# A first unit of two first blocks in place of three, a further unit for the other two, and three edits beside it

## The chip, the cores and the metric

The kernel runs on one core of one Trainium2 chip, in one launch. The metric is device time in microseconds (us); the median of three runs before the change is 285.51 us (285.26 to 285.83).

A core has a matmul engine (PE, with its weight loads as PEld), a vector engine (DVE), an engine for activations (ACT), a general one (POOL) and SP, which issues transfers. Each runs its own instructions strictly in the order in which they were written, and waits on the others through semaphores. Transfers run on 16 DMA engines; here SP's queue carries the inputs and outputs, POOL's queue the weights of the FFN, which are turned from 32-bit into 16-bit floats on the way.

## What is computed

For four batches of eight heads with 768 positions and a head width of 64: block-sparse causal attention, and a gated FFN on the result.

```python
k_chunks = k.reshape(B, H, nc, chunk, D)            # chunks of 32 keys, nc = 24
k_min, k_max = np.min(k_chunks, axis=3), np.max(k_chunks, axis=3)
ub = np.sum(np.maximum(q * k_min, q * k_max), axis=-1)   # a bound for each query and chunk
ub = np.where(causal, ub, -1e9)
top_chunks = np.argsort(ub, axis=-1)[..., -6:]      # six chunks a query
scores = scale * q @ k.T
scores = np.where(sel & (pos[:, None] >= pos[None, :]), scores, -1e9)
attn = softmax(scores) @ v
x = attn.transpose(0, 2, 1, 3).reshape(3072, 512)
out = (sigmoid(x @ w_gate) * (x @ w_val)) @ w_out   # 512 -> 1536 -> 512
```

## The kernel before

**Tiles and units.** The 768 positions of a batch are six blocks of 128. A query of a batch's first block sees at most four chunks, so all that it sees is chosen, and such a *first block* needs only causal attention within 128 keys (`first`). All other blocks need the bounds, the choice of six chunks (`choose`), and attention over all earlier blocks with a mask (`attend`). Work goes by *units* of three blocks, 384 tokens. Unit 0 (`u0`) is the first blocks of batches 0, 1 and 2; `u1` is blocks 1 to 3 of batch 0; `u2` is blocks 4 and 5 of batch 0 and the first block of batch 3; `u3` to `u7` go on through batches 1 to 3. Every unit gets its FFN: `ffn` for `u0` to `u3`, and `ffn_pair` for the pairs `u4`/`u5` and `u6`/`u7`, which uses seven half products in place of eight.

**Names.** A first block's loads are `kf0`, `kf1`, `qf0`, `qf1` (half the heads each) and `vf`; PE turns them (`kfT`, `qfT`), ACT or DVE casts them (`kf16`, `qf16`), PE writes a causal triangle into the score bank (`scm`) and adds the scores (`scf`), ACT takes the exponential (`expf`), PE multiplies by the values (`pvf`), DVE normalizes (`rzf`, `xf`), and PE turns the result (`xpsf`) into `xT`, the FFN's input. For blocks of batch 0 beyond the first, `k0_u1` and the like are loads, `kn`/`qn` a copy into another order, `kT`/`qT` the turns, `kx0`/`kx1` the chunk minima and maxima, `ub_u1` the bounds, `mx`, `ap`, `apt`, `hqm` the choice; `sc`, `exp`, `cm`, `pv`, `x` and `xps` are the attention; `v_0_1` is a load of values and `v16_0_1` its cast on POOL. In the FFN, `g` and `v` are the two products of one of twelve column groups, `tanh` and `hg` their gating, `o0`, `o1`, `o2` thirds of the output projection of one token block, `osb` its copy out of PSUM, `out` the store. `wm` are 24 filler matmuls that keep PE busy early on. `wg`, `wv` and `wo` are the weight transfers, three each.

**The mask.** The extra 64 rows of the score product carry the choice: `hk` holds on these rows a fixed pattern that says which chunk a key belongs to. `pat` makes the pattern, `epat0` and `epat1` spread it to 768 columns, and four `hkp` copies put it into `hk`; every score product reads it.

**Order.** Nothing is scheduled on the chip. The program lists operations with their reads, writes and priorities, and a word list, `ORDER`, made beforehand by a planner, gives the order in which they are written, with the engine of an operation where there is a choice (`@ACT`) and the buffer slots (`:0`). The engines' own orders are the parts of this list. A load into a buffer waits for the last reader of that slot; `o0` of a token block waits for the transfer of the rows of `w_out` that it uses.

```python
def after(i, key, prio):      # a small POOL copy: what follows waits for a landed load
def weights(i, prio, after):  # wg{i}, wv{i}: 512 of 1536 columns each
def weights_out(i, prio, after):  # wo{i}: 4 of 12 row groups
```

`after0` waits for a load of the first block of batch 1, and `after1` for one of batch 2; `wg0` and `wv0` follow the first, the others the second.

Of the kernel before, what the change touches and what calls it, by code (L numbers as in the profile page):

```python
# [94 lines left out]
v10 q3_u1:0 pat0 kcr0 pat kf0_0:0 kf1_0 kf0_1:1 q0_u1 k3_u1 qn_u1_3@DVE:0 k1_u1 tri0 tri qf0_0:2 ident qf1_0 epat0:0  # L95
kfT_0:0 q2_u2:1 k0_u2 kf16_0:1 kxf1:0 qf1_1:3 qn_u1_0:2 kf1_1 ident16 kn_u1_3@DVE:3 wm_0:1 vf_0:4 kn_u1_1@DVE:4 wm_1
hkf1@DVE q2_u1 wm_2 kxf0 qf0_1 kT_u1_1:2 k0_u1 scm_0:3,4 qn_u2_2@POOL:5 kt_u1_1:0 k1_u2 qf0_2:5 hk0_u1_1@ACT qfT_0:5
q1_u2 hkp010@ACT kT_u1_3:6 qf1_2 qf16_0@DVE:6 kt_u1_3@DVE:1 q1_u1 v16_0_0 scf_0:0 kx1_u1_1:1 wm_3 hkf0 kf1_2:0
expf_0_1:1 hk0_u1_3 qT_u1_3:7 expf_0_0 kf0_2 kx0_u1_1 qfT_1:0 qn_u1_2:4 q0_u2 kx0_u1_3 wm_4 kn_u2_0:3 qf_u1_3:0
qT_u1_0:5 k2_u1 pvf_0_0:4 wm_5 hk1_u1_1@ACT qf_u1_0@DVE vf_1:2 pvf_0_1:3 wm_6 kn_u1_0:6 kn_u2_1@DVE:1 vf_2:4  # L100
qm_u1_0@POOL:0 hq1 qf16_1@DVE:0 kT_u1_0:2 k2_u2 kfT_1:7 kcr_f@POOL ap1 qm_u1_3@POOL qn_u1_1:2 scm_1:5,0 kx1_u1_3
kf16_1@DVE:6 after0 qT_u1_2:6 q3_u2 hk1_u1_3 qf_u1_2 scf_1:2 vf1_1:4 rzf_0_1:0 k3_u2 epat1@DVE:1 qT_u1_1:7 wg0
expf_1_0 wm_7 v_0_1:1 wm_8 expf_1_1:3 kn_u1_2@POOL:0 wm_9 v_0_3:3 qm_u1_2 kfT_2:6 kt_u1_0:0 wv0 kx1_u1_0 qf_u1_1
qfT_2:5 v_0_2:0 hq0_u1_0 rzf_0_0:1 kx0_u1_0 kT_u1_2:0 wm_10 after1 qm_u1_1@POOL kf16_2:6 kx0_u1_2 vc_1@ACT xf_0_0:0
wg1 kx1_u1_2 hq0_u1_1 xpsf_0_0:7,0 pvf_1_0:2 scm_2:6,4 wv1 rzf_1_0:1 qf16_2:2 kt_u1_2@DVE:1 xf_1_0:1 scf_2:1 vf1_2:0
hq0 pvf_1_1:5 kcr_u1 wm_11 expf_2_0 xTf_0_0 qn_u2_1@POOL:2 ub_u1:0,2 qn_u2_0@DVE:6 wg2 vc_2@ACT k01_1:0 ap0 expf_2_1:0
rzf_1_1:1 xf_1_1:2 wv2 hkp001@ACT xf_0_1:0 pvf_2_0:7 pvf_2_1:6 qT_u2_0:5 rzf_2_0:0 ubn1_u1:0 wm_12 hkp000@POOL wm_13
ubm1_u1 xpsf_0_1:4 qf_u2_0@DVE:1 wm_14 wm_15 xTf_0_1 hkp011@ACT wm_16 rzf_2_1:1 xpsf_1_1:3 xf_2_1:0 wm_17 wm_18
kn_u2_2@DVE:4 hq1_u1_2@POOL wm_19 xf_2_0:2 xpsf_1_0:2 xpsf_2_1:5 ubn0_u1 wm_20 hq1_u2_0@POOL hk0_u1_2@ACT
hk0_u1_0@POOL ubm0_u1 mx0_u1:0 kn_u2_3:0 wo1 qn_u2_3:6 xTf_1_1@ACT xpsf_2_0:4 xTf_2_0 qT_u2_2:6 xTf_1_0 kT_u2_0:7  # L110
xTf_2_1@ACT qT_u2_1:0 wm_21 ap0_u1 apt0_u1:0 mx1_u1 hqm0_u1_2 k00_1 qf_u2_1@DVE kT_u2_3:4 kt_u2_3:2 qf_u2_2 qT_u2_3:3
qf_u2_3 kT_u2_2:2 g_u0_0:5,0,0 wm_22 tanh_u0_0 v_u0_0:6 hqm0_u1_0 kx0_u2_3 hk1_u1_2@ACT hk1_u2_3 g_u0_1:3,1,1
hq1_u1_1@POOL kx1_u2_3:1 ap1_u1 sc_u1_1_0:0,2 qm_u2_0@POOL:0 tanh_u0_1 v_u0_1:5 hg_u0_0 qm_u2_2@ACT kx1_u2_2
g_u0_2:4,2,2 hq1_u1_0@POOL kt_u2_2@DVE:1 hq0_u1_2@POOL kx1_u2_0 v_u0_2:3 tanh_u0_2 apt1_u1 hq0_u1_3@POOL exp_u1_1_0
g_u0_3:6,3,3 kx0_u2_2 v16_0_1 hg_u0_1 sc_u1_0_1:4,3 wo0 v_u0_3:2 hg_u0_2 tanh_u0_3 hk0_u2_3@ACT hkp110 sc_u1_0_0:0
hk1_u1_0@POOL exp_u1_0_1 g_u0_4:5,0,4 exp_u1_0_0 kx0_u2_0 sc_u1_3_2:6,1 kt_u2_0@DVE:2 sc_u1_2_2:3,0 sc_u1_3_1:4
exp_u1_3_2 sc_u1_2_0:0 qm_u2_1 exp_u1_3_1 kT_u2_1:7 qm_u2_3 v_u0_4:6 exp_u1_2_0 kx1_u2_1 kx0_u2_1 sc_u1_3_0:4 cm_u1_2
g_u0_5:0,1,5 hg_u0_3 exp_u1_3_0 hkp100@POOL v_u0_5:2 kt_u2_1:0 hq1_u2_3 tanh_u0_5 g_u0_6:4,2,6 tanh_u0_4 hq0_u2_1@POOL
hg_u0_5 sc_u1_0_2:7 v_u0_6:0 kcr_u2@POOL exp_u1_0_2 hg_u0_4 cm_u1_3 hqm1_u1_2@ACT sc_u1_1_2:5 cm_u1_0 g_u0_7:2,3,7
v16_0_3 v_u0_7:7 tanh_u0_7 wo2 tanh_u0_6 g_u0_8:6,1,8 hg_u0_7 hq0_u2_3 cm_u1_1 ub_u2:2,4 hq1_u1_3@DVE tanh_u0_8  # L120
hq0_u2_0@POOL exp_u1_2_2 hk1_u2_0@POOL sc_u1_2_1:7 v_u0_8:6 hqm1_u1_0 exp_u1_2_1 k11_1 exp_u1_1_2 g_u0_9:3,0,9
hq1_u2_1@POOL hg_u0_8 v_u0_9:7 tanh_u0_9 sc_u1_1_1:5 g_u0_10:6,3,10 hg_u0_9 ubn1_u2:0 v_u0_10:3 v16_0_2 tanh_u0_10
exp_u1_1_1 g_u0_11:7,1,11 v11 hg_u0_10 pv_u1_3:4 ubn0_u2 tanh_u0_11 pv_u1_2 mx1_u2:0 pv_u1_0:6 hk0_u2_1@ACT
sc_u1_5_2:5,1 v_u0_11:3 hk0_u2_2 exp_u1_5_2 hg_u0_6 hk1_u2_2@ACT wm_23 hg_u0_11 pv_u1_1 sc_u1_6_1:1,3 sc_u1_5_0:2
hq0_u2_2@DVE exp_u1_6_1 sc_u1_7_1:7,0 rz_u1_1:0 sc_u1_5_1:5 x_u1_1:1 exp_u1_7_1 sc_u1_6_0:0 rz_u1_0:0 exp_u1_6_0
sc_u1_4_1:3,2 hkp101 exp_u1_5_0 sc_u1_4_0:1 o0_u0_0:4,0 kcr1 mx0_u2 k10_1 exp_u1_5_1 xps_u1_1:7,1 cm_u1_5 o1_u0_0
hq1_u2_2 ap1_u2 exp_u1_4_1 ap0_u2 sc_u1_7_0:0 x_u1_0:0 sc_u1_6_2:2 o2_u0_0 exp_u1_7_0 apt1_u2:0 exp_u1_6_2
hqm1_u2_0@DVE exp_u1_4_0 xps_u1_0:5 o0_u0_1:3,1 osb_u0_0@DVE cm_u1_4 apt0_u2 out_u0_0 o1_u0_1 cm_u1_6 hqm0_u2_2@ACT
cm_u1_7 sc_u1_4_2:6 pv_u1_5:0 hqm0_u2_0 q01_1:1 exp_u1_4_2 pv_u1_6:2 sc_u1_7_2:1 hqm1_u2_2 kf0_3:5 pv_u1_4 exp_u1_7_2
sc_u2_1_0:4,1 rz_u1_2:0 sc_u2_3_2:6,3 xT_u1_0 sc_u2_3_0:1 exp_u2_1_0 x_u1_2:2 pv_u1_7 o2_u0_1 exp_u2_3_0 cm_u2_1  # L130
rz_u1_3:0 x_u1_3:1 exp_u2_3_2 xT_u1_1 sc_u2_1_1:5 k16_1_2:5 sc_u2_2_0:4,2 kx1_1_3:0 exp_u2_1_1 sc_u2_7_1:0,0
xps_u1_3:1 q10_1 xps_u1_2:2 k16_1_3:3 exp_u2_2_0 sc_u2_3_1:6 k16_1_0@DVE:2 q00_1 o0_u0_2:7,0 osb_u0_1 cm_u2_3 kt_1_3:0
hk0_u2_0@ACT cm_u2_2 o1_u0_2 exp_u2_7_1 xT_u1_3 xT_u1_2@ACT kx0_1_0 o2_u0_2 v_0_4:2 kx1_1_0 g_u1_0:5,0,12 v_u1_0:4
kt_1_0:6 tanh_u1_0 g_u1_1:3,3,13 kx0_1_1 sc_u2_2_1:0 v_0_5:4 v_u1_1:1 exp_u2_2_1 hg_u1_0 q11_1 g_u1_2:2,2,14 tanh_u1_1
# [10 lines left out]
hg_u1_10 hk0_1_1@ACT sc_u2_6_1:3 mx1_u3 o0_u1_0:7,0 hqm0_u3_0@ACT hg_u1_11 o1_u1_0 rz_u2_1:0 ap1_u3 exp_u2_6_0
qf0_u4_1 x_u2_1:0 qfT_3:4 exp_u2_6_1 q00_2:1 cm_u2_6 apt1_u3 sc_u2_6_2:5 hq1_u3_2@ACT hqm0_u3_2 sc_u2_4_2:0 pv_u2_0
hk1_1_0 rz_u2_0:0 exp_u2_6_2 sc_u3_1_1:6,3 qf16_3@DVE:1 exp_u2_4_2 sc_u3_1_0:3 o2_u1_0 x_u2_0:1 cm_u2_4 exp_u2_4_1
kx0_2_2 o0_u1_1:5,1 hk1_1_2 osb_u1_0 exp_u3_1_0 hqm1_u3_0@DVE hk0_1_2 out_u1_0 pv_u2_7:4 kx1_2_3:0 pv_u2_4:0 v_1_3:4
xps_u2_1:2,0 sc_u2_5_1:1,0 v_1_2:1 xT_u2_1@ACT hkp111@POOL hqm1_u3_2@DVE exp_u3_1_1 scf_3:7,3,2 o1_u1_1 q10_2
# [1104 lines left out]
```

## Time and profile before

| | |
|---|---|
| median of three runs | 285.51 us |
| the profiled execution | 285.57 us |
| its span, first to last instruction | 283.7 us |
| PE, DVE, ACT, POOL busy | 95%, 83%, 73%, 41% of the span |
| read from and written to memory | 30.67 and 6.29 MB |

Times in the profile are microseconds from the span's start. A row of a timeline names the start, the duration, the engine, the line of the kernel, the operation, the tile written and the tiles read, and how many instructions are merged (x4). Matmuls are pipelined, so the duration of one (379 ns for 512 columns) is longer than the distance between two starts; distances say what PE can do. A row of a chain of waits gives the start, the length and the work that the end of the kernel hung on. "DMA to landing" is the time from issue until the data is there. The DMA share is a sum over packets in flight, divided by 16 engines, and can pass 1.

### The profile page before, as it was taken

The page shows a single profiled execution, that of the slowest core. Times are in us where ns is not written, and L with a number is a line of the kernel's source. Part 1 is how long each engine was busy: PE and PEld are TensorE (multiplying, and loading weights), DVE is VectorE, ACT ScalarE, POOL GpSimd, SP SyncE. Part 2 cuts the span into 40 slices and gives each one's busy share as a digit, 9 for nine tenths or more (in the row PEclk, how much of TensorE's full clock was granted, in tenths as well). Part 3 has the DMA queues.
Part 4 walks back from the last instruction along what each step waited for, and adds up shares of the span by engine and source line. Part 5 has one row for each costly group of instructions (what it writes and reads, how often), then busy time and mean ns, then how long its engine had stood idle before and what let it go on. Part 6 is the DMA issues. An engine that isn't in the chain of part 4 may idle for free.

```text
span 283.7 us, 7050 instructions
## 1 busy us (share of the span) xinstructions
...
## 2 busy tenths in 40 slices
...
DMA  6999999999999979999720143200001320200014
GB/s 173 254 252 201 196 200 216 167 206 178 229 171 183 199 154 159 217 168 227 166 54 2 31 116 94 64 14 2 0 0 31 104 91 12 76 0 0 2 73 149
DMA packets 130033, 34.26 MB, mean 121 GB/s; under 512 B 118096, under 2 KB 127056, under 8 KB 130000
## 3 DMA queue, kind: packets, MB, share of 16 engines
...
q8 instruction: 20, 0.33, 0.5%
q14 instruction: 13, 0.11, 0.1%
HBM read 30.67 MB, written 6.29 MB: 130 GB/s over the span
## 4 chain that ended last, share of the span: by engine, by line
PE 85%; DVE 4%; ACT 4%; issue 3%; POOL 2%; DMA 1%; DVEq 0%; POOLq 0%
PE o_u L981 22%; PE sc_u L862 11%; PE v_u L950 11%; PE g_u L950 11%; PE pv_u L895 6%; PE suv_u6u L1059 3%; PE sug_u6u L1059 3%; PE ube_u L801 3%; PE suv_u4u L1059 2%; PE sug_u4u L1059 2%; PE srg_u6u L1059 1%; PE srv_u6u L1059 1%; PE srv_u4u L1059 1%; PE srg_u4u L1059 1%; DMA kq_u<-in_q_dram 1%
## 5 line engine op out<-in xcount | busy, mean ns | idle before, releaser
L873 ACT ACTIVATE att_u<-sc_u 128x512 f16<-128x512 f32 (+3 forms) x184 | 90.4, 550 | 17.9 <-PE sc_u L862 17.0
L879 POOL TENSOR_SCALAR_AFFINE_SELECT att_u<-att_u 128x384 f16<-128x384 f16 (+1 forms) x56 | 28.5, 519 | 73.7 <-ACT att_u L873 52.4
L981 PE MATMUL o_u<-wo,hg_u 128*128 128x512 f16 x216 | 52.8, 379 | 0.0
L950 PE MATMUL v_u<-xT_u,wv 128*128 128x384 f16 x192 | 39.1, 326 | 0.1
L950 PE MATMUL g_u<-xT_u,wg 128*128 128x384 f16 x192 | 39.0, 326 | 0.0
L981 PEld LDWEIGHTS <-hg_u 128*128 128x128 f16 x216 | 20.0, 98 | 18.8 <-issue 0.6
L958 ACT ACTIVATE gate_u<-g_u 128x384 f16<-128x384 f32 x48 | 22.9, 494 | 11.0 <-PE g_u L950 9.3
L962 DVE SCALAR_TENSOR_TENSOR hg_u<-gate_u,v_u 128x384 f16<-128x384 f16 x48 | 25.1, 537 | 6.9 <-PE v_u L950 3.9
L862 PE MATMUL sc_u<-hqe,hke 128*128 128x128 f16 (+2 forms) x220 | 29.0, 243 | 0.0
L895 PEld LDWEIGHTS <-att_u 128*128 128x128 f16 x640 | 25.0, 98 | 4.9 <-issue 0.5
L862 PE MATMUL sc_u<-hqo,hko 128*128 128x128 f16 (+2 forms) x220 | 27.4, 243 | 0.0
L895 PE MATMUL pv_u<-v,att_u 128*128 128x65 f16 x640 | 27.2, 193 | 0.1
L950 PEld LDWEIGHTS <-wv 128*128 128x128 f16 x192 | 18.3, 98 | 10.9 <-issue 0.6
L950 PEld LDWEIGHTS <-wg 128*128 128x128 f16 x192 | 18.2, 98 | 10.6 <-issue 0.2
L862 PEld LDWEIGHTS <-hke 128*128 128x128 f16 x220 | 17.2, 98 | 7.3 <-issue 0.4
L862 PEld LDWEIGHTS <-hko 128*128 128x128 f16 x220 | 16.6, 98 | 6.5 <-issue 0.8
L567 POOL CAST v<-v 128x512 f16<-128x512 f32 x23 | 14.9, 662 | 12.4 <-DMA v<-in_v_dram 8.1
L990 ACT ACTIVATE osb_u<-o_u 128x512 f32<-128x512 f32 (+1 forms) x13 | 7.8, 597 | 13.9 <-PE o_u L981 13.9
L981 PE MATMUL o_u<-wo,hgp_u 128*128 128x512 f16 (+1 forms) x72 | 16.2, 370 | 0.0
L914 DVE TENSOR_TENSOR x_u<-pv_u,rz_u 128x384 f16<-128x384 f32 (+1 forms) x28 | 14.8, 531 | 0.4
L1059 PEld LDWEIGHTS <-Sv 128*128 128x128 f16 x96 | 9.0, 98 | 6.2 <-issue 0.3
L824 DVE MAX8 mx_u<-ubn_u 128x8 f32<-128x8 f32 (+16 forms) x152 | 12.6, 158 | 0.1
...
## 6 DMA issues: line engine op xcount, KB each, us to landing
v<-in_v_dram SPq DMA_DIRECT2D x23, 256.0 KB, 4.9
out_dram<-osb_u SPq DMA_DIRECT2D x23, 256.0 KB, 2.3
k<-in_k_dram SPq DMA_DIRECT2D x12, 384.0 KB, 5.8
q<-in_q_dram SPq DMA_DIRECT2D x12, 384.0 KB, 5.5
wg<-in_moe_w_gate_dram POOLq DMA_DIRECT2D x3, 512.0 KB, 10.8
wv<-in_moe_w_val_dram POOLq DMA_DIRECT2D x3, 512.0 KB, 13.4
wo<-in_moe_w_out_dram POOLq DMA_DIRECT2D x3, 512.0 KB, 12.8
kf<-in_k_dram SPq DMA_DIRECT2D x8, 128.0 KB, 3.9
```

Of the source, the lines that this page charges most:

```text
L567: plan.add(f"v16_{b}_{ib}", {POOL: pool(H * D)}, lambda e: nc.gpsimd.tensor_copy(v16[b % 2][:, ib, :, 0:D], at(t)), reads=[t], writes=[("v ...
L824: nc.vector.max(at(mx)[:, e_, j, :], at(ubn)[:, e_, j, 0:max(8, u.seen[j])])
L862: nc.tensor.matmul(at(t)[:, o:o + 128 * m], hk[b % 2][e_][:, p, 128 * jb:128 * jb + 128], hq[u.side][e_][:, p, 128 * x:128 * (x + m)], sta ...
L873: plan.add(f"exp_{u.name}_{h}_{y}", {ACT: act(n)}, lambda e, t=t, att=att, b0=b0, n=n: nc.scalar.activation(at(att)[:, b0:b0 + n], at(t), ...
L879: nc.gpsimd.affine_select(out=dv, in_=dv, compare_op=ALU.is_ge, fill=0.0, base=0, pattern=[[0, u.m], [1, 128]], channel_multiplier=-1)
L895: nc.tensor.matmul(at(pv)[:, last, x, :], at(att)[:, c:c + 128], v16[b % 2][:, jb, h, :], start=(jb == 0), stop=(jb == ib))
L914: plan.add(f"x_{u.name}_{p}", {DVE: dve(u.t)}, lambda e: nc.vector.tensor_tensor(at(x_).rearrange("p a (e d) -> p e a d", e=2), at(pv)[:, ...
L950: nc.tensor.matmul(at(t), w16[:, c, 128 * fb:128 * fb + 128], at(u.xt)[:, c, :], start=(c == 0), stop=(c == 3))
L958: plan.add(f"tanh_{u.name}_{fb}", {ACT: act(T)}, lambda e, g=g, gate=gate: nc.scalar.activation(at(gate), at(g), AF.Tanh, scale=0.5), read ...
L962: plan.add(f"hg_{u.name}_{fb}", {DVE: dve(T)}, lambda e, w_=w_, gate=gate, hg=hg: nc.vector.scalar_tensor_tensor(at(hg), at(gate), 1.0, at ...
L981: nc.tensor.matmul(at(o), hgs[c][1][1]()[:, 128 * tb:128 * tb + 128], wo16[:, fc, lo:hi], start=(c == 0), stop=(c == NFB - 1))
L1059: nc.tensor.matmul(at(t), left[i](c), right[i](c), start=first and c == 0, stop=c == 1, skip_group_check=not first)
```

## The change

Five things change at once, and the order list with them.

1. `u0` is the first blocks of batches 0 and 1 alone (256 tokens); a new unit `u8` holds the first blocks of batches 2 and 3; `u2` loses its third block. Their FFN products have 256 columns in place of 384, and there are three such units in place of two (with `u2`).
2. For the first blocks of batches 2 and 3 the triangle is put on after the exponential, by POOL (`cmf`), where before it was so for batch 3 alone.
3. The pattern for the mask is spread and copied in two column parts, chunks 0 to 7 and 8 to 23, so that `epat0` becomes `epat0a` and `epat0b`, and each `hkp0` an `a` and a `b`; a score product over the first four key blocks reads part `a`, and part `b` only where a key block beyond the fourth is used.
4. `w_out` comes in one transfer (`wo0`) in place of three, and every weight transfer follows `after0`.
5. The order list is a new one throughout, with new engines and slots.

```diff
     units = [
-        Unit(0, [], [(0, 0), (1, 1), (2, 2)]),
+        Unit(0, [], [(0, 0), (1, 1)]),
         Unit(1, [(0, 1), (0, 2), (0, 3)]),
-        Unit(2, [(0, 4), (0, 5)], [(3, 2)]),
+        Unit(2, [(0, 4), (0, 5)]),
...
+        Unit(8, [], [(2, 0), (3, 1)]),
     ]
...
+    PARTS = slice(0, 8), slice(8, NC)
...
+        for y, cut in enumerate(PARTS):
+            n = CH * (cut.stop - cut.start)
+            const(f"epat{o}{'ab'[y]}", {POOL: pool(n), DVE: dve(n, 1, 64), ACT: act(n, False, 64)}, lambda e, o=o, cut=cut: copy(
+                e, at(epat[o])[:, cut], pat[:, o, cut].unsqueeze(2).to_broadcast([64, cut.stop - cut.start, CH])),
+                reads=["pat"], writes=[(epat[o], y)], prio=-2.3)
...
-    def weights_out(i, prio, after):
-        return plan.add(f"wo{i}", {POOL: (760, 760)},
-                 lambda e: nc.gpsimd.dma_start(wo16[:, 4 * i:4 * i + 4, :], wos[:, 4 * i:4 * i + 4, :]),
-                 reads=after, writes=[("wo", i)], prio=prio, dma=(3000, 2048))
+    def weights_out(prio, after):
+        return plan.add("wo0", {POOL: (760, 760)}, lambda e: nc.gpsimd.dma_start(wo16, wos),
+                 reads=after, writes=[("wo", i) for i in range(3)], prio=prio, dma=(9000, 2048))
...
-        masked = b < 3
+        masked = b < 2
...
-                reads += [("hkp", b % 2, e_, p) for b, _, _, _ in u.banks[y]] + [("hq", u.side, e_, p), ("hqm", u.side, e_, p)]
+                reads += [("hkp", b % 2, e_, p, z) for b, jb, _, _ in u.banks[y] for z in range(1 + (jb > 3))] + [("hq", u.side, e_, p), ("hqm", u.side, e_, p)]
...
-            g = ps(f"g_{u.name}_{fb}", "ff", [128, T])
-            w_ = ps(f"v_{u.name}_{fb}", "ff", [128, T])
+            g = ps(f"g_{u.name}_{fb}", "ff", [128, u.w])
+            w_ = ps(f"v_{u.name}_{fb}", "ff", [128, u.w])
...
-    raw_f = {b: load_first(b, -10.0 + b) for b in range(3)}
+    raw_f = {b: load_first(b, -10.0 + b) for b in range(2)}
...
-    after(1, (raw_f[2]["q"], 1), -0.6)
     for i in range(1, 3):
-        weights(i, -0.5 + 0.2 * i, ["after1"])
-    for i in range(3):
-        weights_out(i, 0.3, ["after1"])
+        weights(i, -0.5 + 0.2 * i, ["after0"])
+    weights_out(0.3, ["after0"])
...
     ffn(units[0], 1.0, 0.95)
+    for b, x in units[8].first:
+        raw_f[b] = load_first(b, 0.05)
+        first(units[8], b, x, raw_f[b], 0.5)
+    ffn(units[8], 1.5, 0.5)
...
-    first(units[2], 3, 2, raw_f[3], 2.0)
```

The engines' orders at the start, read out of the two lists up to the first FFN product and a little beyond:

| | before | after |
|---|---|---|
| SP issues ahead of `g_u0_0` | 36 | 28 |
| SP from its 24th issue on, after | | `vf_0 vf_1 q3_u2 k00_1 v_0_3 v_0_2 qf0_2 kf0_2 vf_2 kf1_2 qf1_3 qf1_2 kf0_3 kf1_3 qf0_3 v_0_1 k01_1` |
| POOL around the weights, before | `qm_u1_3 after0 vf1_1 wg0 kn_u1_2 wv0 after1 qm_u1_1 wg1 wv1 vf1_2 qn_u2_1 wg2 wv2` and later `wo1`, `wo0`, `wo2` | |
| POOL around the weights, after | | `after0 tri hkp001b vf1_1 v11 kn_u2_0 qn_u2_2 kn_u1_0 hk1_u1_3 wv0 hk1_u1_1 wv1 v10 wg0 v16_0_0 hq0_u1_3 qn_u1_1 hkp001a kcr_f wg1 wv2 hk0_u1_0 hq0_u1_1 wg2 wo0 vc_1` |
| fillers ahead of `g_u0_0` | 22 of 24 | 24 of 24 |
| PE between `g_u0_0` and the first `o0_u0_0` | all of the `g`/`v` of `u0`, 20 score groups of `u1`, `kT_u2_1`, `ub_u2`, 4 `pv` | all of the `g`/`v` of `u0`, `kT_u2_2`, 7 score groups of `u1` |
| PE from `o0_u0_0` to the first `pv`, after | | `o0_u0_0 sc_u1_2_1 ub_u2 kfT_2 o1_u0_0 sc_u1_1_1 sc_u1_1_2 sc_u1_2_2 sc_u1_3_2 qfT_2 kfT_3 qfT_3 o2_u0_0 pv_u1_2` |
| the last stores | `out_u7_2` (384 columns), `outb_u7_2` (128) | `out_u7_2` (384), `out_u7_0` (512) |

More of the change, by code (lines that the diff above doesn't have):

```diff
@@ L94 @@
 ORDER = """
[L95 to L134, printed above, removed]
@@ L145 @@
[L145 to L149, printed above, removed]
@@ new lines @@
+hkp000a@ACT wm_4 k2_u2 qn_u1_0@DVE:2 wm_5 epat0b@ACT tri0 q2_u2 tri wm_6 hkp001b@POOL kf0_1:3 qT_u1_3:2 kn_u1_3@DVE:3
+k3_u2 scm_0:3,4 vf1_1:4 qf0_1 qf_u1_3:0 hkp011a v11 hkp011b@ACT kf1_1 kfT_0:5 kn_u2_0@POOL:5 k2_u1 kT_u1_3:6
+kf16_0@DVE:6 wm_7 hkp000b@ACT wm_8 q1_u2 kxf1:0 k1_u2 qn_u2_2@POOL:0 hkf0@ACT kx1_u1_1:1 vf_0:4 kn_u1_0@POOL:1
+kx0_u1_3 kt_u1_3:0 vf_1:5 kx1_u1_3 kT_u2_0:7 q3_u2 hk1_u1_3@POOL kt_u1_1@DVE:1 qT_u1_0:2 wm_9 wm_10 qf_u1_0 qfT_0:2
+wv0 qm_u1_0:0 wm_11 hk1_u1_1@POOL qf16_0@DVE:3 kT_u1_0:6 wm_12 wm_13 wv1 qm_u1_3 scf_0:0 expf_0_1:1 v10 kx1_u1_0
```

349 lines of the change are left out of this document (196 added, 153 removed).

## The prediction

> **What bounds the kernel now.** I read the page first, then a table of stretches, then the chain of waits, then the rows around the first product of the FFN.
>
> ```profile
> span 283.7 us, 7050 instructions
> ...
> DMA  6999999999999979999720143200001320200014
> ```
> ```profile
> 0.00:8.00 8.00, 1.09 (x4) 0.71 (x4) 1.42 (x5) 2.28 (x3) 2.30 (x11) 1.00 0.74 185
> 8.00:14.00 6.00, 5.42 (x25) 3.41 (x26) 3.98 (x10) 2.69 (x4) 1.56 (x3) 1.00 1.06 251
> 14.00:20.00 6.00, 5.17 (x48) 3.86 (x47) 5.25 (x13) 4.62 (x11) 3.53 (x7) 1.00 1.13 259
> 20.00:26.00 6.00, 4.97 (x76) 2.90 (x74) 5.78 (x19) 5.45 (x12) 5.93 (x10) 1.00 1.16 208
> 26.00:31.20 5.20, 4.68 (x36) 3.09 (x37) 4.88 (x28) 4.41 (x9) 3.63 (x5) 1.00 1.22 196
> 31.20:53.00 21.80, 21.80 (x210) 14.11 (x209) 15.77 (x55) 15.96 (x39) 14.66 (x25) 1.00 1.24 195
> 53.00:64.60 11.60, 11.60 (x111) 7.19 (x109) 9.61 (x30) 9.19 (x20) 6.17 (x11) 1.00 1.15 196
> ```
>
> The columns are the stretch, its length, the busy time of PE, weight load, DVE, ACT and POOL, granted clock, DMA share and GB/s. Two things are full. From 31.2 us PE is busy in every microsecond shown. And from 8 us the DMA share is above 1.00: the 16 engines never rest in this part, and the page's slices of 7.1 us stay at 9, but for one 7, to about 130 us.
>
> That PE is full with work and not with waiting shows in the spacing of its matmuls.
>
> ```profile
> 33.58 0.65 PE v_u L950 x4
> ...
> 62.05 2.59 PE o_u L981 x12
> ```
>
> Four products of 384 columns take 0.65, so 0.1625 each; twelve of 512 take 2.59, so 0.216. The line through both is 0.42 ns a column and 2.7 ns a matmul, and 256 columns cost 0.109. The body has no idle PE to win back; what can be won lies before the first `g_u0_0`, and anything that makes PE wait later is lost in full. So I ask of each point of the new order: how much PE work stands ahead of it, and when had the old kernel done as much (its par)?
>
> ```profile
> 18.80 0.40 PE L642 MATMUL scf<-qf,kf 64*128 64x128 f16 x8
> 19.13 0.55 PE L700 MATMUL qT_u<-ident,qn_u 128*128 128x128 f32 x3
> 19.51 0.81 PE L1146 MATMUL spare<-ident 128*128 128x512 f16 x3
> 20.16 0.60 PE L603 MATMUL kfT<-ident,kf 128*128 128x128 f32 x4
> 20.59 0.60 PE L603 MATMUL qfT<-ident,qf 128*128 128x128 f32 x4
> ```
>
> From start to start: a turn of a first block 0.43 (20.16 to 20.59), its scores 0.33 (18.80 to 19.13), a filler 0.22. By the line above the triangle is 0.43 (two of 512 columns), a `pvf` 0.12 (four of 65), an `xpsf` 0.11 (two of 128).
>
> **The change, part by part: work.** `scm_2` goes (two matmuls of 512, -0.43); the FFN of the first blocks is 288 products of 256 columns in place of 192 of 384, the same columns and 96 more matmuls, +0.26. Net -0.2. The output projection is as long as before (24 blocks).
>
> **The start.** The five loads of block 2 (4x128 and 256 KB, 0.79 MB) no longer stand ahead of `g_u0_0`, and blocks 2 and 3 are turned behind it. The old order has 22 fillers, the new one all 24 ahead of it; the new one lacks two turns, `scm_2`, one `scf`, two `pvf` and two `xpsf`: 0.43 - 0.86 - 0.43 - 0.33 - 0.24 - 0.22 = -1.65, say -1.7 of PE work. `g_u0_0` began at 31.0, so its par is 29.3.
>
> ```profile
> 9.77 0.47 SPq L530 DMA_DIRECT2D qf<-in_q_dram  x1
> 18.81 0.99 POOL L506 DMA_DIRECT2D wg<-in_moe_w_gate_dram  x1
> 19.81 0.71 POOL L349 COPY kn_u<-kq_u 128x384 f32<-128x384 f32 x1
> 23.99 0.40 POOL L349 COPY qn_u<-kq_u 128x256 f32<-128x256 f32 x1
> 28.57 0.50 POOL L349 COPY hke<-kt_u 64x384 f16<-64x384 f16 x1
> 31.02 0.81 PE L950 MATMUL g_u<-xT_u,wg 128*128 128x384 f16 x4
> ```
> ```profile
> L512 POOL DMA_DIRECT2D wo<-in_moe_w_out_dram x3: 746/786/1106, 29.0 to 43.6; - x3
> ...
> DMA to landing us min/median/max: 8.5/12.8/17.5
> ```
> ```profile
> L561 SPq DMA_DIRECT2D v<-in_v_dram x3: 413/532/7819, 20.2 to 21.3; - x3
> ...
> DMA to landing us min/median/max: 12.6/18.6/24.6
> ```
>
> In the new POOL order the first weight (`wv0`) stands behind `qn_u2_2`, which needs the 16th SP load. The old 16th was issued at 9.77; with a landing of about 3.8 (an estimate; the median of `kf` below is 3.9) it is there at 13.6; then `qn_u2_2` 0.40, `kn_u1_0` 0.71, `hk1_u1_3` 0.50: `wv0` goes out at 15.2, 3.6 us sooner than the old first weight (18.81). But `wg0` is now third. The three `wo` transfers landed at 29.0+17.5=46.5, about 49.2 and 43.6+8.5=52.1: they queue, 2.8 us each. Behind `wv0` and `wv1`, `wg0` lands between 15.2+2+3x2.8=25.6 (the 2 is my allowance for the start) and 31. So `g_u0_0` starts around its par: I count the start as nothing, with -2.5 to +1.5 as ends.
>
> **The output weights in one transfer.** `o0_u0_0` now needs all of `w_out`. Ahead of it stand, beyond the old kernel's `g_u0_0`, the 24 `g`/`v` groups (96 matmuls at 0.109, 10.4), seven score groups of `u1` (3072 columns, 1.3) and `kT_u2_2` (0.2), less the 1.7 above: 10.2, par 41.2. The old kernel sent nine weight transfers in 52.1-18.8=33.3 us. Nine from 15.2 end between 15.2+2+9x2.8=42.4 and 15.2+33.3=48.5. I take 47, near the old kernel's whole, since SP's queue is as full: PE stands some 5.8 us there (ends 1.2 and 7.3). POOL's own cost of the one transfer isn't shown; between 0.79 (as one of the three) and 2.4 (three times that). I take 0.79; at 2.4 `vc_1`, queued behind it, makes `g_u0_0` later, and this wait shorter by as much.
>
> **The loads of the further unit.** All SP loads of `u8` wait in the same queue, ahead of `v_0_1`, and `pv_u1_2`, the first value product in the PE order, needs `v_0_1`. How fast SP's queue moves beside the weights shows above: three value loads issued by 21.3 needed 12.6, 18.6 and 24.6 us. The pipe is full, so bytes set the time.
>
> ```profile
> v<-in_v_dram SPq DMA_DIRECT2D x23, 256.0 KB, 4.9
> ...
> k<-in_k_dram SPq DMA_DIRECT2D x12, 384.0 KB, 5.8
> ...
> wg<-in_moe_w_gate_dram POOLq DMA_DIRECT2D x3, 512.0 KB, 10.8
> ...
> kf<-in_k_dram SPq DMA_DIRECT2D x8, 128.0 KB, 3.9
> ...
> kq_u<-in_q_dram SPq DMA_DIRECT2D x4, 192.0 KB, 4.0
> ...
> kq_u<-in_q_dram SPq DMA_DIRECT2D x4, 128.0 KB, 3.8
> ```
>
> Up to `v_0_1` the new SP order has 8x192 (`u1`), 8x128 (`u2`), 16x128 (`kf` and `qf` of four first blocks), three `vf` and three `v` of 256, one `k` piece of 384: 6528 KB; with nine weights of 512, 11136 KB, or 11.40 MB. The old kernel had moved 8x185+6x251+6x259+6x208+5.2x196+21.8x195 = 11.06 MB by 53.0, and 196 GB/s after it: 11.40 MB at 54.8. I take 54.6, ends 53 and 57 (the mix of packets). Its cast on POOL:
>
> ```profile
> L567 POOL CAST v<-v 128x512 f16<-128x512 f32 x23 | 14.9, 662 | 12.4 <-DMA v<-in_v_dram 8.1
> ```
>
> so `pv_u1_2` starts at 55.3. PE work ahead of it, beyond the 10.2: three `o` groups of 0.86 (2.6), five more score groups (1536 columns, 0.6), the bounds of `u2` (1.0; the row below gives 2.0 for half the products of three units, ends counted, so at most 1.3 for one), four turns of blocks 2 and 3 (1.7): 16.1, par 47.1. PE is then 8.2 us behind the old kernel, the 5.8 included.
>
> ```profile
> L801 PE MATMUL ubo_u<-qf_u,kcr 64*32 64x256 f32 x24 | 2.0, 386 | 0.0
> ```
>
> Behind the waiting `pv_u1_2` stand all of `u1`'s second half and the FFN of `u8`; PE was full there before, so nothing is caught up. Ends: 5.8 (the loads hidden behind the weights) and 10.
>
> **The rest.**
>
> ```profile
> L958 ACT ACTIVATE gate_u<-g_u 128x384 f16<-128x384 f32 x48 | 22.9, 494 | 11.0 <-PE g_u L950 9.3
> ...
> L990 ACT ACTIVATE osb_u<-o_u 128x512 f32<-128x512 f32 (+1 forms) x13 | 7.8, 597 | 13.9 <-PE o_u L981 13.9
> ```
>
> These two give 0.8 ns a column and about 0.19 fixed, so twelve more `tanh` cost ACT 2.2 us in the body and, if DVE's fixed part is alike (an estimate), twelve more `hg` as much there. Both lie beside PE's columns, which are as many as before; without that cover it is 2.2, in the range. The pattern in parts is two more fills and four more copies, by the same fixed part 1.1 over three engines, beside loads that end later. The end changes: the old kernel ends with a DVE copy of 128 columns and 64 KB, the new one with an ACT copy of 512 (0.60 above) and 256 KB.
>
> ```profile
> 280.58 0.29 DVE L991 TENSOR_SCALAR osb_u<-ob_u 128x128 f32<-128x128 f32 x1 [5.65 <-PE ob_u L981]
> ```
> ```profile
> out_dram<-osb_u SPq DMA_DIRECT2D x23, 256.0 KB, 2.3
> ...
> out_dram<-osb_u SPq DMA_DIRECT2D x1, 64.0 KB, 1.6
> ```
>
> 0.3 and 0.7: +1.0, or 0 if the two last outputs overlap.
>
> **Sum.** The profiled execution took 285.57 with a span of 283.7 and stands 0.06 over the median. 285.57 + 8.2 - 0.2 + 1.0 = 294.6; I say 294, its own range 290 to 298.
>
> The Trainium skill (DMA: Bandwidth & Descriptors, Anatomy of one DMA) gives such a transfer 2.0 us plus its bytes at 436 GB/s; by it one transfer in place of three would save 4.0, and an estimate by that page would be 290.6. The landings above, 2.8 apart for 512 KB, show no 2 us paid one after the other.
>
> **Rivals.** (a) The start wins and the transfers keep up: `wg0` at 25.6, `g_u0_0` at 26.8, 2.5 under par, and all of `w_out` before 38.7. Then 285.57-2.5+0.8=283.9. For it: the 0.79 MB less and a start where PE does 1.09 in 8 us. Against: the share above 1.00. It decides if `w_out` lands before 41. (b) Only the weights wait, the loads are hidden behind them: 285.57+5.8+0.8=292.2. (c) The waits cool PE. Three fillers took 1.46 early (row below) and 0.81 at 19.5: PE runs at half speed after idleness. A stand of 5.8 could bring that back for about 4 us as at 8.4 to 12.9, +2: 296.6.
>
> ```profile
> 8.44 1.46 PE spare L1146 x3
> ```
>
> The Trainium skill (TensorE: Matmul & The Clock Gate, Part 1) has the clock halve after an idle window of 3.4 us; the early row agrees with a cold start, and no run here shows a mid-kernel one.
>
> **Chances.** Forecast 50, (b) 20, (c) 16, (a) 10, no difference within 0.2% (what a measurement here can tell from none) 4. So faster 0.10, same 0.04, slower 0.86. Range 288 to 298: it holds (b), the forecast and (c), and leaves out (a).
>
> **What would show it.** Right: the first `o_u` after 45 with PE idle before it, the first `pv_u` at 53 to 57 waiting on POOL's cast, PE full from about 57, DMA share over 1.00 to there. Wrong: a first `o_u` at 41 without a gap, or no PE gap over 1 us after the first `g_u`; also a first `g_u` before 28.

## The result and the profile after

| | before | after |
|---|---|---|
| median of the runs | 285.67 us (285.26 to 287.2) | 295.86 us (294.69 to 296.13) |
| the profiled execution | 285.57 us | 295.63 us |
| its span | 283.7 us | 293.9 us |

The 285.67 is over four runs, the 285.51 given ahead over the first three of them. The ratio is 1.0339 with a 95% interval of 1.0291 to 1.0386: slower, as forecast, by 10.1 us in the profiled executions where the sum gave 9.0. The stretches of the profile after, two of those shown of before and two finer ones (stretch, length, busy PE, weight load, DVE, ACT, POOL, granted clock, DMA share, GB/s):

```profile
31.20:53.00 21.80, 17.20 (x172) 13.39 (x171) 14.15 (x64) 10.36 (x27) 8.43 (x16) 1.00 1.23 211
53.00:64.60 11.60, 10.38 (x146) 7.25 (x144) 8.42 (x36) 9.15 (x22) 6.62 (x12) 1.00 1.18 167
60.00:65.00 5.00, 4.72 (x70) 3.60 (x69) 4.46 (x15) 4.87 (x13) 3.52 (x8) 1.00 1.17 186
65.00:70.00 5.00, 4.85 (x60) 4.30 (x58) 4.86 (x10) 4.85 (x11) 3.00 (x5) 1.00 1.06 209
```

PE, which was busy for 21.80 of 21.80 us before, is busy for 17.20, beside the same full DMA engines (1.23). Where most of the other 4.6 go stands in the timeline of PE; the bracket at the end is the idle time ahead of a row and what ended it:

```profile
43.02 0.60 PE L960 MATMUL v_u<-xT_u,wv 128*128 128x256 f16 x4
45.36 1.04 PE L991 MATMUL o_u<-wo,hg_u 128*128 128x512 f16 x4 [1.74 <-DMA wo<-in_moe_w_out_dram]
46.23 0.33 PE L872 MATMUL sc_u<-hqe,hke 128*128 128x384 f16 x1
...
50.09 0.63 PE L613 MATMUL kfT<-ident,kf 128*128 128x128 f32 x4 [2.51 <-ACT vf L349]
...
54.54 0.19 PE L905 MATMUL pv_u<-v,att_u 128*128 128x65 f16 x1
55.68 0.40 PE L905 MATMUL pv_u<-v,att_u 128*128 128x65 f16 x8 [0.94 <-POOL v L577]
```

Three waits in a row: `o0_u0_0` for `w_out`, `kfT_2` for block 2's own loads (the cast on ACT that the row names is another work; `kf1_2` landed at 50.00, 0.09 ahead of the turn), the rest of the first value product for the cast of `v_0_1`. The last two are one thing, for both loads stand in SP's queue. The timeline of SP's issues:

```profile
24.79 0.34 SPq L561 DMA_DIRECT2D k<-in_k_dram  x1
25.23 17.04 SPq L571 DMA_DIRECT2D v<-in_v_dram  x2
42.38 2.94 SPq L540 DMA_DIRECT2D qf<-in_q_dram  x1
...
49.40 0.51 SPq L540 DMA_DIRECT2D qf<-in_q_dram  x1
50.01 0.45 SPq L571 DMA_DIRECT2D v<-in_v_dram  x1
```

From 25.2 to 42.4 SP hands out two loads, and all of `u8`'s stand behind them. Before that it handed out none from 16.3 to 24.8, when `k00_1`, the first row, waited 8.4 us for its buffer; this load, in pieces of 128 bytes, landed at 45.50. The chain of waits goes that way, not through the weights:

```profile
25.23 21.06 DMA v<-in_v_dram
46.29 0.02 issue
...
50.01 4.78 DMA v<-in_v_dram
54.78 0.02 issue
...
54.90 0.73 POOL v L577
```

Two groups to set against those of before: POOL's value casts now idle 18.5 us for their loads (8.1 before), and the gating's 60 activations cost ACT 2.0 us more.

```profile
L968 ACT ACTIVATE gate_u<-g_u 128x256 f16<-128x256 f32 (+1 forms) x60 | 24.9, 430 | 14.9 <-PE g_u L960 14.7
...
L577 POOL CAST v<-v 128x512 f16<-128x512 f32 x23 | 14.3, 632 | 22.3 <-DMA v<-in_v_dram 18.5
```

**A measure for what follows.** PE's *lost time* at an instant is the start of the last matmul up to it, less the spacing that all matmuls ahead of that one take on a full PE (the line of the prediction for 16-bit products, the turns at 0.109 each, products that run side by side at their share of the spacing). Ahead of the last matmul this work is 261.49 us before and 261.14 after; with that matmul, of 128 columns before and 512 after, it is 261.55 and 261.36. Worked out from the traces:

| lost, us | at the first `g_u` | 60 | 75 | 100 | the last matmul | from its end to the span's end |
|---|---|---|---|---|---|---|
| before | 14.95 | 15.16 | 15.16 | 15.60 | 18.76 | 3.24 |
| after | 15.95 | 23.59 | 24.78 | 24.92 | 28.55 | 3.86 |

Of the difference of the spans, 10.2, 9.6 is made up by 75 us, nearly all of it after the first `g_u`: 24.78 - 15.95 = 8.83 against 0.21.

### The profile page after: what moved, and what is told of

It is laid out like the page before. It is cut to its first block, busy times and chain, and to the rows that moved or that the text cites. A ratio compares the mean times of both kernels' runs of the same rounds, so it can differ in the third digit from the quotient of the medians.

```text
span 293.9 us, 7275 instructions
## 1 busy us (share of the span) xinstructions
PE 271.6 (92%) x2696; PEld 178.8 (61%) x2696; DVE 235.8 (80%) x654; ACT 211.3 (72%) x456; POOL 109.6 (37%) x184
## 4 chain that ended last, share of the span: by engine, by line
PE 73%; DMA 10%; ACT 5%; DVE 4%; POOL 3%; SPq 2%; issue 1%; POOLq 0%; ACTq 0%; DVEq 0%
PE o_u L991 18%; PE sc_u L872 10%; PE g_u L960 9%; PE v_u L960 9%; DMA v<-in_v_dram 9%; PE pv_u L905 6%; PE suv_u6u L1069 3%; PE sug_u6u L1069 3%; PE suv_u4u L1069 2%; PE sug_u4u L1069 2%; PE ube_u L811 2%; DMA kf<-in_k_dram 1%; PE srv_u6u L1069 1%; PE srg_u6u L1069 1%; SPq L551 1%
## 5 line engine op out<-in xcount | busy, mean ns | idle before, releaser
L889 POOL TENSOR_SCALAR_AFFINE_SELECT att_u<-att_u 128x384 f16<-128x384 f16 (+1 forms) x56 | 30.5, 556 | 76.2 <-ACT att_u L883 42.4
L960 PE MATMUL g_u<-xT_u,wg 128*128 128x256 f16 (+1 forms) x240 | 41.3, 294 | 0.6 <-ACT xT_u L349 0.6
L960 PE MATMUL v_u<-xT_u,wv 128*128 128x256 f16 (+1 forms) x240 | 41.2, 294 | 0.0
L968 ACT ACTIVATE gate_u<-g_u 128x256 f16<-128x256 f32 (+1 forms) x60 | 24.9, 430 | 14.9 <-PE g_u L960 14.7
L972 DVE SCALAR_TENSOR_TENSOR hg_u<-gate_u,v_u 128x256 f16<-128x256 f16 (+1 forms) x60 | 26.5, 458 | 7.3 <-ACT gate_u L968 3.8
L905 PE MATMUL pv_u<-v,att_u 128*128 128x65 f16 x640 | 28.6, 194 | 1.4 <-POOL v L577 0.9
L960 PEld LDWEIGHTS <-wg 128*128 128x128 f16 x240 | 22.6, 98 | 8.2 <-issue 1.4
L960 PEld LDWEIGHTS <-wv 128*128 128x128 f16 x240 | 22.9, 98 | 6.8 <-issue 0.4
L577 POOL CAST v<-v 128x512 f16<-128x512 f32 x23 | 14.3, 632 | 22.3 <-DMA v<-in_v_dram 18.5
L1000 ACT ACTIVATE osb_u<-o_u 128x512 f32<-128x512 f32 (+1 forms) x16 | 9.5, 596 | 14.6 <-PE o_u L991 14.6
L1154 PE MATMUL spare<-ident 128*128 128x512 f16 x24 | 8.1, 443 | 5.1 <-DVE ident L496 5.1
```

The source lines that it names most:

```text
L577: plan.add(f"v16_{b}_{ib}", {POOL: pool(H * D)}, lambda e: nc.gpsimd.tensor_copy(v16[b % 2][:, ib, :, 0:D], at(t)), reads=[t], writes=[("v ...
L889: nc.gpsimd.affine_select(out=dv, in_=dv, compare_op=ALU.is_ge, fill=0.0, base=0, pattern=[[0, u.m], [1, 128]], channel_multiplier=-1)
L905: nc.tensor.matmul(at(pv)[:, last, x, :], at(att)[:, c:c + 128], v16[b % 2][:, jb, h, :], start=(jb == 0), stop=(jb == ib))
L960: nc.tensor.matmul(at(t), w16[:, c, 128 * fb:128 * fb + 128], at(u.xt)[:, c, 0:u.w], start=(c == 0), stop=(c == 3))
L968: plan.add(f"tanh_{u.name}_{fb}", {ACT: act(u.w)}, lambda e, g=g, gate=gate: nc.scalar.activation(at(gate), at(g), AF.Tanh, scale=0.5), re ...
L972: plan.add(f"hg_{u.name}_{fb}", {DVE: dve(u.w)}, lambda e, w_=w_, gate=gate, hg=hg: nc.vector.scalar_tensor_tensor(at(hg), at(gate), 1.0, ...
```

## Experiments

The theories: A, the full queues set it, with `v_0_1` behind `u8`'s loads as the last arrival; B, the single transfer of `w_out`; C, the start, the pattern parts or the narrower products.

**e1: `w_out` in three transfers again.**

```diff
-        return plan.add("wo0", {POOL: (760, 760)}, lambda e: nc.gpsimd.dma_start(wo16, wos),
+        return plan.add(f"wo{i}", {POOL: (760, 760)},
+                 lambda e: nc.gpsimd.dma_start(wo16[:, 4 * i:4 * i + 4, :], wos[:, 4 * i:4 * i + 4, :]),
...
-wo0
+wo0 wo1 wo2
```

> The changed kernel with the output weights in three transfers again, issued back to back where the one transfer stood; nothing else moves. Theory A (the loads behind one another in the full queues set the loss, and the last of them that matters is v_0_1): the first value product still starts at 54.5 to 56, PE's wait ahead of the first o_u may shrink by up to its 1.9 us, but it is given back before the first value product; time within 1 us of the changed kernel's 295.9. Theory B (the single transfer is the loss, because the first o_u waits for all of w_out): the first o_u comes 1.9 us sooner or more and the time falls by 1.9 to 2.8 us, to 293 to 294. Theory C (start, pattern parts and the narrower FFN products): no change.

296.38 us, ratio 1.0393 (1.0355 to 1.0431). The first `o_u` came at 43.55 without a wait, 1.8 sooner, and all of it was gone again at the turn: PE's timeline and the stretches of e1,

```profile
49.89 1.08 PE L613 MATMUL kfT<-ident,kf 128*128 128x128 f32 x4 [4.12 <-ACT att_u L883]
50.77 1.91 PE L991 MATMUL o_u<-wo,hg_u 128*128 128x512 f16 x4
```
```profile
47.00:50.50 3.50, 0.61 (x3) 0.64 (x4) 0.00 (x0) 0.90 (x2) 3.44 (x7) 0.81 1.15 240
50.50:55.00 4.50, 4.50 (x19) 3.04 (x18) 2.94 (x14) 0.81 (x2) 0.04 (x2) 0.50 1.36 184
```

B falls: the same stand, now in one piece of 4.1 us (for `kf1_2`, which landed at 49.80, and not for the exponential that the row names). And something that the profile of after lacks: behind it PE ran at a granted clock of 0.50, four `o_u` in 1.91 us where they took 1.04, and the first value product came at 56.85, later than A had it. Rival (c) of the prediction is real, in this neighbour; e13, below, takes it out again, and the time stays within the changed kernel's interval then too.

**e5 and e6: two of the edits alone, put on the kernel before** (for e6 with the code of the change's third point).

```diff
 e5
-wo1 ... wo0 ... wo2
+wo0
 e6
-epat0:0 ... epat1@DVE:1 ... hkp000@POOL
+epat0a:0 epat0b ... epat1a@DVE:1 epat1b@DVE ... hkp000a@POOL hkp000b@POOL
```

> The kernel before with its output weights in one transfer, where the first of its three stood. Theory A (a transfer of 1.5 MB lands when its bytes have come through, whatever the number of transfers, and the wait in the changed kernel came from PE arriving sooner): the first o_u, at 52.9 in the kernel before, moves by less than 1 us; time within 0.3% of before. Theory B (one transfer costs time by itself, since the first o_u has to wait for its last byte): slower by 1 to 3 us.

> The kernel before with the mask pattern built and copied in column parts (two more fills, four more copies; the rest as it was). Theory A: hidden beside loads, within 0.3% of before. Theory C (the parts delay the start): slower by up to 1.1 us.

e5: 285.02 us, ratio 0.9998 (0.9983 to 1.0013). e6: 285.37, ratio 1.0006 (0.9977 to 1.0035). The rows of tile `wo` in e5 (duration in ns; nobody waited, though the transfer landed 23.6 us after its issue):

```profile
L509 POOL DMA_DIRECT2D wo<-in_moe_w_out_dram x1: 1024/1024/1024, 28.4 to 28.4; - x1
...
DMA to landing us min/median/max: 23.6/23.6/23.6
```

One transfer costs POOL 1.02 us, and the time nothing. What is left of the change is the new units with their order. Three pieces of it were not run alone: the triangle behind the exponential for block 2, the start of the weights behind `after0`, and the narrower products, which the count of matmuls prices at 0.26 us.

**e2: the load `k00_1` behind `v_0_1`.**

```diff
-k00_1:0 wo0 ... v_0_3:2 ... v_0_2:1 ... qf0_2 ... v_0_1:1 k01_1
+wo0 ... v_0_3:2 ... v_0_2:1 ... qf0_2 ... v_0_1:1 k00_1:0 k01_1
```

> The changed kernel with the load k00_1 (384 KB, not needed before block 1) moved in SP's queue from ahead of v_0_3 to behind v_0_1. Theory A by bytes alone: 0.39 MB fewer ahead of v_0_1 at 196 GB/s lands it 2.0 us sooner (52.8) and the time falls by about 2 us, to 294. Rival (the two queues share the engines packet by packet, and k00_1's small pieces held SP's queue back to the good of the weights): SP's loads ahead of v_0_1 land much sooner, before 45, the weights later, w_out at 47 to 50 instead of 45.3; PE waits 2 to 5 us more ahead of the first o_u and hardly at all ahead of the first value product; the time moves by -2 to +1 us.

298.77 us, ratio 1.0464 (1.0433 to 1.0495): 3 us worse. With 0.39 MB fewer ahead of it, `v_0_1` landed at 55.42, not at 52.8 but 0.6 later than in the changed kernel, so the bytes alone do not set the landing. The rival had the mechanism right, and the sizes too small: `w_out` came later than its 47 to 50, and the time lies outside its -2 to +1. PE's timeline of e2:

```profile
51.28 1.89 PE L989 MATMUL o_u<-wo,hg_u 128*128 128x512 f16 x4 [5.21 <-DMA wo<-in_moe_w_out_dram]
```

`w_out` landed at 51.2 in place of 45.3, PE stood 5.2 us for it and came out of it at half clock. The packets say why. Between 35 and 40 us both queues moved the same number of packets. In the changed kernel, with 944 on each, SP's were `k00_1`'s of 128 bytes, 0.12 MB, and the weights' of 1024 bytes, 0.96 MB. With `k00_1` away, with 780 on each, SP's were of 256 bytes, 0.19 MB, and the weights got 0.78 MB. The Trainium skill (DMA: Bandwidth & Descriptors, Queues, rings and completion order) has each engine go round between the queues packet by packet; these counts agree.

**e7 to e14: `v_0_1` ahead of `u8`'s loads.** e7 moves the load, and the turns of blocks 2 and 3 behind the first value products:

```diff
 SP
-k00_1 v_0_3 v_0_2 qf0_2 kf0_2 vf_2 kf1_2 qf1_3 qf1_2 kf0_3 kf1_3 qf0_3 v_0_1 k01_1
+k00_1 v_0_3 v_0_2 v_0_1 qf0_2 kf0_2 vf_2 kf1_2 qf1_3 qf1_2 kf0_3 kf1_3 qf0_3 k01_1
 PE, behind ub_u2
-kfT_2 o1_u0_0 sc_u1_1_1 sc_u1_1_2 sc_u1_2_2 sc_u1_3_2 qfT_2 kfT_3 qfT_3 o2_u0_0 pv_u1_2 scf_2 pv_u1_0 pv_u1_3 scf_3 pv_u1_1 sc_u1_5_2 o0_u0_1
+o1_u0_0 sc_u1_1_1 sc_u1_1_2 sc_u1_2_2 sc_u1_3_2 o2_u0_0 pv_u1_2 pv_u1_0 pv_u1_3 pv_u1_1 sc_u1_5_2 o0_u0_1 kfT_2 xps_u1_1 qfT_2 o1_u0_1 kfT_3 qfT_3
```

> The changed kernel with v_0_1 loaded right behind v_0_2, ahead of all loads of u8, and the turns, scores and values of blocks 2 and 3 moved on PE to behind the first value products of u1 (order alone; the work is the same). Theory A (u8's loads ahead of v_0_1 are the larger part of the loss): v_0_1 lands at 48 to 49.5, the first value product starts at 49 to 51, no wait over 1 us between the first o_u and there, and the time falls by 3.5 to 6 us, to 290 to 292; the 1.9 us ahead of the first o_u stay. Theory B (the weights are the loss): within 1 us of 295.9. Theory C (start, pattern parts, narrower products): within 1 us of 295.9.

299.96 us, ratio 1.0522 (1.0504 to 1.054). The first half came as A had it, and a little sooner: `v_0_1` at 47.6, the first value product at 48.54 in place of 54.54, lost time 17.8 there in place of 22.0. The second did not: by 75 us 28.9 was lost. ACT stood 3.7 us for the first turn with the exponentials of `u1` queued behind it, so the time went from one wait into the next, and from 59.2 to 62.6 the granted clock was 0.50. So e7 tells where the wait goes, not what the loads cost; e8 and e10 put the work from 45 us on in an order fitted to the landings, with and without the early `v_0_1`.

```diff
 PE, behind o0_u0_0, e8 (SP as in e7)
+sc_u1_1_2 sc_u1_2_2 sc_u1_3_2 ub_u2 o1_u0_0 sc_u1_1_1 o2_u0_0 sc_u1_2_1 o0_u0_1 o1_u0_1 kfT_2 pv_u1_0 pv_u1_2 sc_u1_5_0 pv_u1_3 qfT_2
 e10 (SP as in the changed kernel)
+sc_u1_1_1 o1_u0_0 ub_u2 sc_u1_1_2 sc_u1_2_2 sc_u1_3_2 kfT_2 o2_u0_0 o0_u0_1 sc_u1_2_1 qfT_3 qfT_2 kfT_3 pv_u1_2
```

> As e7_v_first (v_0_1 loaded ahead of all loads of u8), but the instructions of u1's attention, of blocks 2 and 3 and of the first output projection are put in an order that fits these landings: the projection's other groups are pulled ahead of the turns of block 2, and ACT isn't left waiting behind a turn. Theory A (the landing of v_0_1 behind u8's loads costs time, and e7 lost its gain only to the order behind it): by adding up the durations of the e7 trace along this order the first g_u of u8 starts at 61.4 instead of 66.4, and the time falls by 4 to 5 us from the changed kernel's 295.9, to 290.5 to 292. Rival D (u8's own chain of loads, turns, exponentials and casts is the bound, whatever v_0_1 does): first g_u of u8 not before 65, time 295 or more.

> The changed kernel with all its loads as they are, in the same order and from the same places, and only the order of PE, ACT, DVE and POOL from 45 us on fitted to their landings (o_u groups of the first projection pulled ahead of the turns). By adding up durations the first g_u of u8 starts at 64.2 instead of 66.4 and the time falls by about 3 us, to 293. Theory A: this is less than e8 by 1.5 us, since v_0_1 still lands at 55. Rival D: as much as e8 or more.

296.5 us, ratio 1.0391 (1.035 to 1.0432), and 300.41, ratio 1.0523 (1.0483 to 1.0564): both miss in time. But the first `g_u` of `u8` came at 61.99 in e8, where rival D had it not before 65, and at 65.10 in e10 (66.35 in the changed kernel). The lost time at 100 us was 21.09 in e8 and 23.75 in e10, against 24.92. Counted from the first `g_u`, e8 had gained 3.8 there and e10, with the loads unmoved, 1.8: about half of e8's gain may be the order's, and the two orders differ. At 150 the lost time was 25.98 and 30.31. e8 lost it from 101 to 115 us, where PE's waits ended with ACT's work (2.3 us of them scores that waited for exponentials). e10 lost it from 112 to 118, with the clock at 0.50 from 114.6 to 118.0. e11 and e12 keep everything from the end of `u8`'s FFN on in the changed kernel's places.

> As e8 (v_0_1 ahead of u8's loads, the order from 45 us on fitted to the landings), but every instruction from the last products of u8's FFN on stays in the place that the changed kernel gives it, so that the 3.8 us which e8 had gained at 100 us (PE's lost time 21.1 there against 24.9) aren't given back by a new order of u2's scores at 101 to 117. Theory A: the first g_u of u8 starts at 61 to 62.5, of u1's FFN at 79 to 80.5, and the gain of about 4 us lasts to the end: 291 to 292.5. Rival E (what is won here is lost again to the exponentials or the loads behind it, whatever the order): PE's lost time at 150 us no less than the changed kernel's 25.9, time 295 or more.

> As e10 (all loads where the changed kernel has them, only the order from 45 us on fitted to them), with everything from the last products of u8's FFN on in the changed kernel's places. By adding up durations 2.1 us less than the changed kernel: 293.8 (293 to 294.5). Theory A: between e11 and the changed kernel, and 1.5 to 2.5 us over e11; rival (order is all): equal to e11 within 0.7.

295.75 us, ratio 1.0371 (1.0356 to 1.0387), and 304.84, ratio 1.0697 (1.0673 to 1.0721). At 60 us e11 had lost 19.61 and e12 21.37, the changed kernel 23.59. At 150 us e11 had lost 26.25, which with its time is what rival E said. Each had run into a load taken up too early, and behind that into a granted clock of 0.50, e11 for 3.4 us and e12 for 10.2. In e12 POOL stood 8.1 us for a value load, with DVE and PE behind it; e11's waits between 56 and 66 us (who waits for whom, us in all, times, longest):

```profile
DVE kx L583 <- issue: 2.7, 1, 2.7
PE xpsf L688 <- DVE xf L681: 2.5, 3, 2.2
```

e14 is e11 with that mended.

> As e11 (v_0_1 ahead of u8's loads, order from 45 us to the last products of u8's FFN fitted, the rest in the changed kernel's places), refitted to the landings that e8 showed, so that no engine takes up a piece of block 1 before its load is there (in e11 DVE stood 2.7 us for k11_1 with block 3's division queued behind it, and PE 2.4 us for that). Theory A: first g_u of u8 at 60 to 61.5, of u1's FFN at 79.5 to 81 (the changed kernel: 66.4 and 84.3), PE's lost time at 100 and at 150 us 20.5 to 22 and 21.5 to 23 (24.9 and 25.9), the time 3 to 4.5 us under the changed kernel's 295.9: 291.5 to 293. Rival E (lost again to what follows, whatever the order): 295 or more.

294.57 us, ratio 1.0326 (1.0299 to 1.0353). In the trace the gain is there: from the first `g_u` to 100 us PE lost 22.96 - 18.16 = 4.80, against 24.92 - 15.95 = 8.97, a gain of 4.2, and it still stood at 150. The time fell by 1.3 only, and the interval overlaps the changed kernel's. It lies between what A and what E said, and the lost time (22.96 at 100 us, 23.90 at 150) above A's range. In the profiled run 2.2 of the gain went before the first `g_u` (18.16 against 15.95; last section) and 1.0 after 150 us, 0.9 of it in one wait of a `g` product for an exponential. What the other runs lost isn't known: three of the five had a granted clock of 1.00 over the whole run, and took 293.84, 294.15 and 294.95. So A is shown as to where PE stands and for what, but no run got the 3 to 4 us of time back, and how much of the 4.2 is the load's and how much the order's is open.

**e13: e1 with spare products in its wait.**

```diff
+    warm = ps("warm", "wm", [128, 4, 128])
+    for i in range(14):
+        plan.add(f"warm_{i}", pe(512 / 2.4 + 2.4), lambda e: nc.tensor.matmul(
+            at(warm), ident16, ident16.unsqueeze(1).to_broadcast([128, 4, 128]), start=True, stop=True),
...
-kfT_2:5
+warm_0:5 warm_1 warm_2 warm_3 warm_4 warm_5 warm_6 warm_7 warm_8 warm_9 warm_10 warm_11 warm_12 warm_13 kfT_2:5
```

> e1 (w_out in three transfers, PE's wait ahead of the first turn of block 2 is 4.4 us, granted clock 0.50 in 50.5 to 55) with 14 spare products of 512 columns, 3.0 us, put into that wait; nothing reads them. If an idle PE loses its clock there: granted clock 1.00 in 50.5 to 55, the o_u and score groups behind the wait at 0.22 a matmul instead of 0.43, and the time falls by 1.5 to 2.5 us against e1's 296.4, to 294 to 295. If the clock has another cause: no change, or longer by what the products overrun the wait (0 to 0.5 us).

295.45 us, ratio 1.0361 (1.0331 to 1.0391). The stretches of e13:

```profile
47.00:50.50 3.50, 2.05 (x10) 0.72 (x8) 0.00 (x0) 0.05 (x1) 3.50 (x7) 1.00 0.98 220
50.50:55.00 4.50, 4.02 (x27) 2.79 (x28) 3.36 (x20) 2.57 (x7) 1.03 (x3) 1.00 1.20 222
```

The clock stayed at 1.00 where it was 0.50, and so it did in all four runs of e13 (0.99 in all four of e1, taken over the whole run); so idleness had taken it. The time fell by 0.9, less than expected and within the intervals. At 65 us e13 had lost 21.93 and spent 3.02 on the spare products, together 24.95; e1 had lost 24.89. In e13 PE stood 1.08 us for the cast of `v_0_1`, a wait that e1 lacks: e1's slow stretch had covered it.

**e9: the old end.**

```diff
-o2b_u7_2 ... osbb_u7_2@DVE outb_u7_2 o2_u7_0 osb_u7_2 out_u7_2 osb_u7_0 out_u7_0
+o2_u7_0 osb_u7_0 out_u7_0 o2_u7_2 osb_u7_2 out_u7_2 o2b_u7_2 osbb_u7_2@DVE outb_u7_2
```

> The changed kernel with the last output block's two parts in the old order again (512 columns of row block 0 first, the 128-column part of row block 2 as the last store). All theories: the stretch from PE's last matmul to the end of the span falls from 4.0 to about 3.2 us, and the time by 0.8 us (0 to 1.0), to 295.1.

295.37 us, ratio 1.0354 (1.033 to 1.0379); from PE's end to the span's end 3.75 in place of 3.86 (the 4.0 that the expectation starts from ends the last product of 512 columns 0.2 after its start, where the profile has 0.38). The order of the last stores is worth 0.1 here: two ACT copies still stand one behind the other.

## Why the forecast held, and where it was off

**Work:** -0.2 forecast, 261.36 - 261.55 = -0.2 by the matmuls of the traces, at the prediction's own price for each.

**Start:** counted as nothing, within -2.5 and +1.5. `g_u0_0` came at 30.47, 1.2 over its par; the lost time there is 1.0 more. `wv0` went out at 14.83 (15.2) and `wg0`, the third, landed at 29.33, inside its bounds; what `g_u0_0` waited for last was ACT's copy of `xT`.

**Output weights:** they landed at 45.3 (47 taken) and PE was there at 43.5 (par 41.2), so the stand is 1.7 to 1.9 in place of 5.8. The term was sized too large, and it did not matter: what it left over, the next wait took. POOL paid 1.03 us for the issue (0.79 taken).

**Loads of the further unit:** `v_0_1` landed at 54.78 (54.6), the cast took 0.72 (0.66), the value products went on at 55.68 (55.3), with 23.1 lost against 15.1 before: 8.0 behind (8.2). The bytes in order gave this number, with luck: 11.82 MB had moved by then and not 11.40, and faster than in the old kernel, and the same sum is 2.6 off for e2. Nine of `u8`'s ten loads stood ahead of `v_0_1`, as the sum counts them, and not all. The split was different too: of the 8.0, 1.0 was lost to the first `g_u`, 2.7 from there to the first `o_u` and 4.3 behind it, where the forecast had 0, 5.8 and 2.4. I had counted block 2's turn as work, and it was itself a wait for a load of `u8`, 2.5 us.

**Nothing caught up:** true, but neither was PE full from 57, and this is the step that failed in size. Between 55.7 and 75 us another 1.65 was lost. The rows of 60 to 70 us show ACT busy for 4.87 and 4.85 of 5 us: `u1`'s exponentials and those of blocks 2 and 3, late together, made ACT the bound for ten microseconds. That is a reading of the rows; no run took exponentials away.

**End:** +1.0 forecast, 3.86 - 3.24 = 0.6.

Together 8.0 + 1.65 - 0.2 + 0.6, and 0.2 for what PE lost more from 75 us on: 10.2, the difference of the spans. The forecast had 8.2 - 0.2 + 1.0 = 9.0; what it missed is the loss behind 55.7 us, less what it had too large at the end.

**The rivals.** (a) needed `w_out` before 41; it came at 45.3. (b), only the weights wait, falls with e1. (c) did not happen in the runs of the changed kernel, whose granted clock is 1.00, but it did in the profiled runs of e1, e2, e7, e9 to e12 and e14; the last section says how near it was. The Trainium skill gives a transfer a fixed 2 us (DMA: Bandwidth & Descriptors, Anatomy of one DMA), and the prediction's 290.6 counts it three times before and once after. e5 shows no such saving, and in e1 the third of three landed at 44.9 where the single one landed at 45.3: here queued transfers do not pay it one after another.
